# Twelve float32r products of a hidden tile, ordered by contraction piece instead of by operand pair

## The chip, the cores and the metric

The kernel runs on one core of a Trainium2 chip. The metric is the device time of one execution in microseconds (us). Three runs of the kernel before took 601.49, 601.64 and 602.29 us; the median is 601.64 us. For a measurement of this kernel, a difference under about 0.2% (1.2 us) is no difference.

## What is computed

Three layers follow one another. The first is chunked attention with eight memory slots (batch 4, 8 heads, 768 positions, head size 64). Its output, seen as 3072 tokens of 512 features, goes through a rational activation layer. The result goes through a soft mixture of experts.

```python
def _moe_ref(x, w_in, w_out, a, b):
    h = x @ w_in                      # 3072x512 @ 512x2048
    h2 = h * h
    h3 = h2 * h
    P = a[0] + a[1] * h + a[2] * h2 + a[3] * h3
    Q = 1.0 + np.abs(b[0]) * np.abs(h) + np.abs(b[1]) * h2
    g = P / (Q + 1e-06)
    return (g @ w_out).astype(np.float32)
```

The change touches `h = x @ w_in` alone.

## The kernel before, in words

The 3072 tokens are cut into six blocks of 512, and the 2048 hidden features into 8 steps of 256. So there are 48 steps, and each makes one h tile: 128 partitions by two halves of 512 tokens, in two PSUM banks. Two h tiles are alive at a time (pool `ps_h`, two buffers): the tile of the next step is computed while the activation works on that of the present one.

The product is made in float32r, in three parts. x is split into a high part `xh` and a low part `xl`, and `w_in` into `wh` and `wl`; h is the sum of `wh*xh`, `wh*xl` and `wl*xh`. The contraction is 512 long, that is four pieces `c` of 128. So a half of an h tile takes 3 x 4 = 12 matmuls, which accumulate in one bank (`h_part`, the matmul stands in line 321), and the kernel makes 48 x 2 x 12 = 1152 of them. In each, `ww[:, c, ...]` (128x128) is the operand that is loaded into TensorE and `xx[:, c, :]` (128x512) the one that is streamed. Before the change the twelve come in three groups of four: `wh*xh` for all c, then `wh*xl` for all c, then `wl*xh` for all c.

The parts come from elsewhere, and late in some places:

- `xh` and `xl` of a block are made by `attention`, in four slices of tokens, each over all four pieces. ScalarE copies a slice out of PSUM as `xh` (line 237), and VectorE then subtracts it from the same PSUM tile to make `xl` (line 238). Before the first h tile of a new block is computed (in step 7 of the block before), the rest of the attention is emitted.
- `wh` and `wl` of a step are made once, in block 0: ScalarE rounds the converted weight to `wh` (line 304), VectorE makes `wl` from the difference (line 305).

TensorE also makes the transposes of the activation result (line 347, copied out by ScalarE in line 348), the logits (line 340), the attention (lines 164, 201, 214, 233), and in block 0 a product of `w_out` with `phi` (lines 416, 424). All of those but line 340 write to three PSUM banks of the pool `ps_m`, shown as tile `m`. The activation is done by ScalarE (lines 540, 541, 543, 559, 560), VectorE (542, 553, 554, 570, 571) and GpSimd (517). Line 540 is the first reader of a finished h tile. The steps' lists of words (`KN`) say in which order the parts of a step are emitted: `h0` and `h1` are the two halves, `at` a slice of attention, `p0` and `p1` the transposes. Behind the first stage, a scheduler lays out each engine's instructions ahead of time: by the order of emission, but with an instruction that isn't ready by its own estimate passed over for one that is. On the chip each engine then goes strictly by that layout.

Of the kernel before, what the change touches and what calls it, by code (L numbers as in the profile page):

```python
# [44 lines left out]
def tile_chunk_attention__rational__soft_moe(  # L45
# [30 lines left out]
    NC = DM // P  # L76
# [238 lines left out]
    def h_part(step, tile_, f2):  # L315
        b, i = divmod(step, NSTEP)
        (wh, wl), (xh, xl) = win[i], xt[b]
        n = 0
        for ww, xx in ((wh, xh), (wh, xl), (wl, xh)):
            for c in range(NC):  # L320
                PE.matmul(tile_[:, f2, :], lhsT=ww[:, c, f2 * P:f2 * P + P], rhs=xx[:, c, :],  # L321
                          start=(n == 0), stop=(n == 3 * NC - 1))
                n += 1
# [143 lines left out]

    hs[0] = ps_h("h", [P, 2, BLK])
    h_part(0, hs[0], 0)
    h_part(0, hs[0], 1)  # L470
    state = {"att": None}

# [49 lines left out]
    def run_step(kk, what):  # L522
# [5 lines left out]
        elif what in ("h0", "h1"):  # L528
            if nxt < total:
                if what == "h0":  # L530
                    if nxt % NSTEP == 0:
                        while state["att"] is not None:
                            slice_()
                    hs[nxt] = ps_h("h", [P, 2, BLK])
                h_part(nxt, hs[nxt], int(what[1]))
# [231 lines left out]
```

## Time and profile before

| | |
|---|---|
| median of three runs | 601.64 us |
| span of the profiled execution, first to last instruction | 599.9 us |
| TensorE matmul busy | 541.6 us (90%) |
| TensorE weight load busy | 382.6 us (64%) |
| VectorE busy | 455.1 us (76%) |
| ScalarE busy | 417.3 us (70%) |
| GpSimd busy | 125.3 us (21%) |

The profile is of one execution. Its span runs from the first to the last instruction; the metric's 601.64 us is 1.7 us more, for what lies around it. In the trace, a matmul of this kernel shows as two records: one on PEld (the load of its 128x128 operand into TensorE) and one on PE (the streaming of the other operand and the drain of the result). Records on PE overlap, since the next product starts before the last one has drained: what a product costs in a row of them is the distance from its start to that of the next.

### The profile page before, as it was taken

Reading aid. Unit: us, or ns where it says so; the run is one execution under the profiler, and the core shown is the slowest. Engines: PE = TensorE matmul, PEld = TensorE weight load, DVE = VectorE, ACT = ScalarE, POOL = GpSimd, SP = SyncE. Lnnn points to the kernel's source line nnn. Section 1 sums busy time; section 2 is a strip of 40 time slices with the busy share of each in tenths; the row PEclk is TensorE's granted clock in tenths of the full one; section 3 lists DMA queues with packets and bytes.
Section 4 is the critical chain, followed back from the end, with each engine's and each line's share of the span. In section 5 each row is a group of like instructions: output and inputs, shape, how many; then the busy total and the mean of one; then the engine's idle time right before and its main releaser. Section 6 shows DMA issues by size and latency. Waiting matters only on the chain.

```text
span 599.9 us, 13580 instructions
## 1 busy us (share of the span) xinstructions
PE 541.6 (90%) x5898; PEld 382.6 (64%) x5898; DVE 455.1 (76%) x561; ACT 417.3 (70%) x542; POOL 125.3 (21%) x65
## 2 busy tenths in 40 slices
PE   2679899989999999999999999999999999779982
PEld 2567766657767777677776777766777576326241
DVE  4667999988987988978889698896987968711032
ACT  2468999987877868778687777777787869510032
POOL 0000132113313133131331313132232225200000
PEclk9779999989999999999999999999999999889996
DMA  7975987230221223212122022210274334799949
GB/s 298 413 277 188 350 293 261 80 132 0 108 72 32 76 71 107 71 29 79 72 107 69 7 103 73 106 68 5 106 272 157 134 107 174 283 352 410 409 185 360
DMA packets 21755, 97.41 MB, mean 162 GB/s; under 512 B 3136, under 2 KB 3136, under 8 KB 16704
## 3 DMA queue, kind: packets, MB, share of 16 engines
q1 hardware_dynamic: 19728, 92.28, 41.8%
q0 software_dynamic: 1152, 4.19, 1.7%
q8 instruction: 46, 0.75, 0.5%
q10 hardware_dynamic: 816, 0.07, 0.1%
q14 instruction: 13, 0.11, 0.0%
HBM read 86.05 MB, written 10.49 MB: 161 GB/s over the span
## 4 chain that ended last, share of the span: by engine, by line
PE 53%; ACT 19%; DVE 13%; DMA 5%; issue 5%; POOL 2%; SPq 0%; ACTq 0%; DVEq 0%; POOLq 0%
PE h L321 27%; PE m L398 4%; ACT S L540 4%; ACT S L541 3%; PE m L347 3%; ACT g L348 3%; PE lg L340 3%; PE m L214 3%; DVE T L553 3%; PE h L640 2%; PE m L233 2%; POOL S L517 2%; PE m L201 2%; DMA xt<-in_kw_dram 2%; DVE T L554 2%
## 5 line engine op out<-in xcount | busy, mean ns | idle before, releaser
L321 PE MATMUL h<-xt,win 128*128 128x512 f32 x1152 | 294.2, 403 | 7.2 <-ACT win L304 5.1
L321 PEld LDWEIGHTS h<-xt,win 128*128 128x128 f32 x1152 | 210.7, 190 | 54.9 <-ACT win L304 7.7
L517 POOL TENSOR_TENSOR S<-S,S 128x1024 f32<-128x1024 f32 (+1 forms) x49 | 118.9, 2428 | 315.9 <-DVE S L542 302.9
L540 ACT ACTIVATE S<-h,ctab 128x1024 f32<-128x1024 f32 (+1 forms) x49 | 54.0, 1102 | 57.5 <-PE h L321 55.4
L542 DVE SCALAR_TENSOR_TENSOR S<-S,S 128x1024 f32<-128x1024 f32 (+1 forms) x49 | 58.8, 1199 | 41.6 <-ACT S L541 41.4
L553 DVE TENSOR_TENSOR T<-T,h 128x1024 f32<-128x1024 f32 (+1 forms) x49 | 58.4, 1191 | 6.7 <-ACT T L543 6.7
L570 DVE SCALAR_TENSOR_TENSOR T<-T,ctab,S 128x1024 f32<-128x1024 f32 (+1 forms) x49 | 63.3, 1294 | 0.0
L571 DVE SCALAR_TENSOR_TENSOR T<-S,T 128x1024 f32<-128x1024 f32 (+1 forms) x49 | 59.8, 1220 | 3.2 <-POOL S L517 0.5
L347 PEld LDWEIGHTS m<-ident,T 128*128 128x128 f32 x384 | 44.1, 144 | 28.2 <-issue 14.2
L554 DVE SCALAR_TENSOR_TENSOR T<-T,ctab,h 128x1024 f32<-128x1024 f32 (+1 forms) x49 | 61.2, 1250 | 0.7
L543 ACT ACTIVATE T<-h,ctab 128x1024 f32<-128x1024 f32 (+1 forms) x49 | 59.3, 1210 | 0.0
L560 ACT ACTIVATE S<-S,ctab 128x1024 f32<-128x1024 f32 (+1 forms) x49 | 55.9, 1141 | 0.8
L559 ACT ACTIVATE S<-S 128x1024 f32<-128x1024 f32 (+1 forms) x49 | 51.8, 1056 | 6.8 <-DVE S L542 5.0
L348 ACT ACTIVATE g<-m 128x512 f32<-128x512 f32 x96 | 53.6, 605 | 3.1 <-PE m L347 2.9
L347 PE MATMUL m<-ident,T 128*128 128x128 f32 x384 | 54.2, 281 | 1.4 <-DVE a L185 1.2
L541 ACT ACTIVATE S<-h,ctab 128x1024 f32<-128x1024 f32 (+1 forms) x49 | 54.3, 1107 | 0.5 <-DVE T L570 0.5
L340 PE MATMUL lg<-T,wp 128*32 128x512 f32 x192 | 39.9, 614 | 5.4 <-DVE T L571 5.4
L398 PE MATMUL m<-g,ptok 128*32 128x512 f32 x192 | 23.5, 634 | 0.4 <-ACT ptok L390 0.4
L186 ACT ACTIVATE a<-a 128x512 f32<-128x512 f32 x22 | 13.9, 643 | 14.1 <-DVE a L185 14.1
L214 PE MATMUL m<-v,a 64*32 64x64 f32 x1408 | 20.5, 229 | 3.0 <-issue 2.8
L238 DVE TENSOR_TENSOR xt<-m,xt 128x512 fp32r<-128x512 f32 x24 | 16.3, 687 | 7.9 <-ACT xt L237 7.8
L214 PEld LDWEIGHTS m<-v,a 64*32 64x32 f32 x1408 | 17.1, 108 | 7.4 <-issue 4.6
(158 smaller groups left out, 595.6 us busy)
## 6 DMA issues: line engine op xcount, KB each, us to landing
win<-in_moe_w_dram SPq DMA_DIRECT2D x32, 512.0 KB, 6.0
k<-in_kw_dram SPq DMA_DIRECT2D x11, 1024.0 KB, 7.5
v<-in_vw_dram SPq DMA_DIRECT2D x11, 1024.0 KB, 5.4
g<-in_moe_w_in_dram SPq DMA_DIRECT2D x8, 1024.0 KB, 6.2
g<-in_moe_w_out_dram SPq DMA_DIRECT2D x8, 1024.0 KB, 8.1
out_dram<-win SPq DMA_DIRECT2D x12, 512.0 KB, 5.0
q<-in_qw_dram SPq DMA_DIRECT2D x11, 512.0 KB, 3.9
T<-in_moe_w_dram SPq DMA_DIRECT2D x10, 512.0 KB, 9.7
```

The source lines that it names most:

```text
L321: PE.matmul(tile_[:, f2, :], lhsT=ww[:, c, f2 * P:f2 * P + P], rhs=xx[:, c, :], start=(n == 0), stop=(n == 3 * NC - 1))
L347: PE.transpose(pb[:, m, f2 * P:f2 * P + P], t_[:, f2, tt * P:tt * P + P], ident)
L348: ACT.activation(gts[b, qd][:, 2 * part:2 * part + 2, 2 * P * o:2 * P * o + 2 * P], pb, AF.Copy)
L517: POOL.tensor_tensor(out[:, o], q[:, o], w[:, o], ALU.mult)
L540: ACT.activation(s[:, o], hh[:, o], AF.Abs, scale=b0)
L541: ACT.activation(y[:, o], hh[:, o], AF.Square, scale=rb1)
L542: DVE.scalar_tensor_tensor(s[:, o], y[:, o], QC, s[:, o], ALU.add, ALU.add)
L543: ACT.activation(t[:, o], hh[:, o], AF.Identity, bias=a2, scale=a3)
L553: DVE.tensor_tensor(t[:, o], t[:, o], hh[:, o], ALU.mult)
L554: behind[kk] = DVE.scalar_tensor_tensor(t[:, o], t[:, o], a1, hh[:, o], ALU.add, ALU.mult).ins
L570: DVE.scalar_tensor_tensor(t[:, o], t[:, o], a0, w[:, o], ALU.add, ALU.mult)
L571: DVE.scalar_tensor_tensor(t[:, o], e[:, o], 2.0, t[:, o], ALU.subtract, ALU.mult, reverse0=True)
```

## The change

The two loops around the matmul change places: the piece `c` of the contraction is the outer loop, and the three pairs are the inner one. The twelve products, their operands and the bank are the same; their order is `wh*xh`, `wh*xl`, `wl*xh` for c = 0, then the same for c = 1, 2 and 3.

```diff
--- before.py
+++ after.py
@@ -316,8 +316,8 @@
         b, i = divmod(step, NSTEP)
         (wh, wl), (xh, xl) = win[i], xt[b]
         n = 0
-        for ww, xx in ((wh, xh), (wh, xl), (wl, xh)):
-            for c in range(NC):
+        for c in range(NC):
+            for ww, xx in ((wh, xh), (wh, xl), (wl, xh)):
                 PE.matmul(tile_[:, f2, :], lhsT=ww[:, c, f2 * P:f2 * P + P], rhs=xx[:, c, :],
                           start=(n == 0), stop=(n == 3 * NC - 1))
                 n += 1
```

## Rows read from the trace of the kernel before

**Rows 1.** Stretches: us, busy and count by engine, granted clock, DMA share, GB/s.

```profile
36.70:142.00 105.30, 96.58 (x988) 72.95 (x989) 91.98 (x100) 90.81 (x114) 21.00 (x14) 0.96 0.57 201
142.00:218.00 76.00, 75.59 (x885) 54.84 (x883) 63.92 (x77) 59.79 (x75) 19.22 (x8) 1.00 0.20 71
218.00:294.00 76.00, 75.75 (x890) 55.28 (x885) 65.36 (x79) 59.55 (x78) 19.27 (x8) 1.00 0.21 71
```

**Rows 2.** Waits of ScalarE, 142 to 508 us: total, times, longest.

```profile
ACT S L540 <- PE h L321: 54.0, 25, 3.6
```

**Rows 3.** Waits of ScalarE in block 0, 36.7 to 142 us.

```profile
ACT S L540 <- PE h L321: 1.5, 1, 1.5
```

**Rows 4.** The page's costliest groups: busy, mean ns, idle before; the products' own.

```profile
L321 PE MATMUL h<-xt,win 128*128 128x512 f32 x1152 | 294.2, 403 | 7.2 <-ACT win L304 5.1
L321 PEld LDWEIGHTS h<-xt,win 128*128 128x128 f32 x1152 | 210.7, 190 | 54.9 <-ACT win L304 7.7
```

**Rows 5.** Timeline of PE: start us, duration us; single products, and a long row.

```profile
225.77 0.50 PE L321 MATMUL h<-xt,win 128*128 128x512 f32 x1
...
226.11 0.40 PE L321 MATMUL h<-xt,win 128*128 128x512 f32 x1
...
139.62 6.74 PE L321 MATMUL h<-xt,win 128*128 128x512 f32 x29
```

**Rows 6.** Groups by shape, line 698 (tile m): loads and matmuls.

```profile
L698 PE MATMUL m<-s,call 32*128 32x256 f32 x48 | 8.8, 402 | 0.5 <-DVE win L705 0.5
...
L698 PEld LDWEIGHTS m<-s,call 32*128 32x128 f32 x48 | 6.8, 184 | 1.2 <-DVE win L705 0.9
```

**Rows 7.** Timeline of PE, the second and the ninth product of the first half tile.

```profile
37.29 0.63 PE L321 MATMUL h<-xt,win 128*128 128x512 f32 x1
...
40.28 0.63 PE L321 MATMUL h<-xt,win 128*128 128x512 f32 x1
```

**Rows 8.** The stretch that holds both, with the granted clock.

```profile
36.70:40.70 4.00, 4.00 (x9) 3.13 (x10) 2.94 (x3) 2.08 (x2) 0.73 (x1) 0.50 0.33 55
```

**Rows 9.** Timeline around the first h tile of block 2 (in brackets: idle, releaser).

```profile
218.19 0.63 ACT L237 ACTIVATE xt<-m 128x512 fp32r<-128x512 f32 x1
...
219.29 5.76 PE L321 MATMUL h<-xt,win 128*128 128x512 f32 x24
219.50 0.68 DVE L238 TENSOR_TENSOR xt<-m,xt 128x512 fp32r<-128x512 f32 x1
...
220.24 4.39 PEld L321 LDWEIGHTS h<-xt,win 128*128 128x128 f32 x20 [0.21 <-DVE xt L238]
220.70 0.64 ACT L348 ACTIVATE g<-m 128x512 f32<-128x512 f32 x1
...
222.22 0.65 ACT L348 ACTIVATE g<-m 128x512 f32<-128x512 f32 x1
...
225.15 1.12 ACT L540 ACTIVATE S<-h,ctab 128x1024 f32<-128x1024 f32 x1 [2.28 <-PE h L321]
```

**Rows 10.** The second and the fifth product of that h tile, alone.

```profile
219.60 0.39 PE L321 MATMUL h<-xt,win 128*128 128x512 f32 x1
...
220.30 0.45 PE L321 MATMUL h<-xt,win 128*128 128x512 f32 x1
```

**Rows 11.** Timeline of block 0, step 7, and the first h tile of block 1.

```profile
128.51 1.46 PE L321 MATMUL h<-xt,win 128*128 128x512 f32 x3 [0.45 <-ACT win L304]
...
130.16 1.41 PE L321 MATMUL h<-xt,win 128*128 128x512 f32 x5
...
131.14 1.28 DVE L238 TENSOR_TENSOR xt<-m,xt 128x512 fp32r<-128x512 f32 x2
...
135.73 2.58 DVE L305 TENSOR_TENSOR win<-g,win 128x1024 fp32r<-128x1024 f32 x1
...
138.36 9.36 PE L321 MATMUL h<-xt,win 128*128 128x512 f32 x40 [0.47 <-DVE win L305]
...
142.32 1.12 ACT L540 ACTIVATE S<-h,ctab 128x1024 f32<-128x1024 f32 x1 [1.86 <-PE h L321]
```

**Rows 12.** Timeline of block 0, step 3.

```profile
69.27 1.23 DVE L305 TENSOR_TENSOR win<-g,win 128x1024 fp32r<-128x1024 f32 x1
69.29 1.89 PE L321 MATMUL h<-xt,win 128*128 128x512 f32 x7 [2.36 <-ACT win L304]
...
71.11 1.48 PE L214 MATMUL m<-v,a 64*32 64x64 f32 x128
```

**Rows 13.** Timeline of VectorE just before the first h tile of all.

```profile
35.94 1.43 DVE L238 TENSOR_TENSOR xt<-m,xt 128x512 fp32r<-128x512 f32 x2 [1.35 <-ACT xt L237]
```

## The prediction

> **What bounds the kernel now.** First I read the stretches, each engine's busy time in each. From 142 us on, the kernel repeats itself block by block in 76 us, and TensorE is busy in 75.59 and 75.75 of 76.0 us, at the full granted clock, while VectorE and ScalarE have 11 to 16 us to spare [rows 1]. Then the waits: from 142 to 508 us the longest wait of ScalarE is for a finished h tile, 25 times and 54.0 us in sum [rows 2]. So in blocks 1 to 5 the products of the h tile are the bound, and what TensorE loses there the kernel loses. Block 0 is another thing: 105.3 us, TensorE idle in 8.7 of them, and ScalarE waited for an h tile just once, for 1.5 us [rows 1, 3]. There the weights are converted, and TensorE has some slack.
>
> Last I read what one product costs. There are 1152, each with a load of its own: 1152 load records of 190 ns beside 1152 matmuls [rows 4]. In an undisturbed row, 29 products take 6.74 us from the first's start to the last's end; less the last one's own record of 0.39 us, 28 distances take 6.35, or 0.227 us from start to start [rows 5, 10]. A load of 0.19 us fits into that; it runs beside the product before. Only the second product of a row pays: it starts 0.34 us after the first (225.77 to 226.11), 0.113 more than the pace [rows 5].
>
> **The change part by part.** It removes and adds no instruction. It does two things.
>
> *Equal operands in a row.* In each group of three the second product has the loaded operand of the first, so 4 of 12, 384 of 1152, could do without a load. Nothing in the edit takes the load out: it is the same matmul call, which brings its load. The nearest row is line 698, where two matmuls after one another in the code have the same loaded operand: 48 matmul records, 48 load records [rows 6]. It is near but not equal, since such a plain f32 product shows as two matmul records with a load each, so equal loads aren't next to each other. I take the loads to stay and the pace to stay 0.227: no gain. The other bound is what a dropped load could give. At half clock the products come (40.28 - 37.29) / 7 = 0.427 us apart [rows 7, 8]; if all of it is streaming, it is 0.2136 at the full clock, and 0.013 of the 0.227 is not streaming. 384 x 0.013 = 5.0 us, and the second product of a row would save 0.113 as well. With a row per step (48) that is 5.4 us more, with a row per half (96) 10.8. So between 0 and -15.8 us; I take 0, the row with a load for each matmul being nearest.
>
> Here a page speaks for a gain. The Trainium skill (TensorE: Matmul & The Clock Gate, Step-by-step: what each phase is for) says that weights stay put over many matmuls, and that load and compute are separate so that one can load once and multiply repeatedly; by that the sum would be 4.35 - 10.4 = -6.05 us. No row here shows a matmul without its load.
>
> *Operands needed earlier.* The first `xl` was needed by the fifth product and is now needed by the second; the first `wl` was needed by the ninth and is now needed by the third. That matters where they arrive late. Products queue in order, so those behind the waiting one wait too.
>
> Block starts 2 to 5 (four, alike; one stands in the rows). The first product starts at 219.29 with `xh` just ready, the second at 219.60; VectorE makes the last `xl` from 219.50 to 220.18, and the first product that reads it, the fifth, starts at 220.30, right after its load was held by that [rows 9, 10]. `xl` was thus already the last to arrive, hidden under four products. After the change the second product takes that place: 220.30 instead of 219.60, so three products come out from under the cover, 0.70 us. The tile ends that much later, ScalarE is waiting for it already (2.28 us) [rows 9], and TensorE has no idle time in the block to give back [rows 1]. 4 x 0.70 = 2.8 us. Block start 1 pays nothing: its `xl` was done at 132.42, its first product comes behind 138.36 [rows 11].
>
> Step 7 of block 0. `wh` let the products begin at 128.51; eight (3 + 5) ran; `wl` was made only from 135.73 to 138.31, and 40 products then followed without a break [rows 11]. Now just two can run ahead, so six more stand behind 138.36: 6 x 0.227 = 1.36 us. ScalarE waits for the following tile (1.86 us before 142.32), and there the TensorE-bound part begins, so I count it in full.
>
> The first half tile of all: the last `xl` ends at 37.37 [rows 13], the second product started at 37.29 [rows 7]; with 0.11 from the end of `xl` to the product, +0.19 us.
>
> Steps 3 to 6 of block 0 (alike, one shown): the products begin at 69.29, `wl` is done at 70.50 [rows 12]. The third product would have come at 69.29 + 0.34 + 0.23 = 69.86 and now comes at 70.61, +0.75; four times that is 3.0 us. I cost it at nothing, because in block 0 ScalarE doesn't wait for h tiles [rows 3] and TensorE has other work to put in between, as the 128 small attention products at 71.11. Without this cover it is +3.0. Steps 1 and 2 have their `wl` in time. Buffers are freed as before, since the last product of a half reads `wl` and `xh` in either order; DMA queues don't move.
>
> The sum: 2.8 + 1.36 + 0.19 = +4.35 us. The profiled execution spans 599.9 us, the runs' median is 1.7 us more for what lies around it; 599.9 + 1.7 + 4.35 = 606.0 us. The bounds of this case are +1.4 (block starts recovered elsewhere) and +7.35 (steps 3 to 6 uncovered): 603.0 to 609.0.
>
> **The rivals.**
>
> *Nothing measurable: the scheduler fills the new gap.* It lays out TensorE's work by estimated readiness; in block 0 it cut rows of products apart for other work [rows 11, 12]. If it puts other work after the first product at the block starts, the gap is used and only the broken row costs 4 x 0.113 = 0.45; if the backlog of step 7 finds slack as well, what is left is 0.5 us: 602.1. Against it: at 219.3 to 220.2 the three `m` banks have readers to come (line 238 until 220.18, line 348 at 220.70 and 222.22 [rows 9]), so transposes and attention have nowhere to write.
>
> *Faster: the load is dropped or costs nothing when repeated.* Place: every second product of a group of three. Price: -5.0 - 5.4 = -10.4 us against +4.35 of waits, 595.6 us; it decides as soon as a repeated load saves more than 4.35 / 384 = 11 ns. For it: the pace is 0.013 us above streaming, and something must take that. Against it: loads equal matmuls in number wherever I look [rows 4, 6].
>
> *Faster by a new layout.* The dependences of two products in each half move, and the layout of all later work follows from the estimate. If each of 48 steps had one broken row fewer, 48 x 0.113 = 5.4 us come back, more than the waits: 600.6 us. As well it could be a break more, 611.4. Nothing in the trace prefers a side.
>
> **How the numbers follow.** A measurement can tell 0.2%, 1.2 us, from no change. My forecast, waits uncovered, has 0.60 and lies wholly on the slower side (603.0 to 609.0). Nothing measurable: 0.20. The dropped load: 0.08. The new layout: 0.08 faster, 0.04 slower. So faster 0.16, same 0.20, slower 0.64. The range must leave out at most 0.2: I leave out the dropped load and the slow layout (0.12) and reach down into the fast layout, to 599.5, and up to 609.0.
>
> **What the profile will show.** Right: 1152 loads beside 1152 products, a pace of 0.227 in undisturbed rows; at the starts of blocks 2 to 5 the second product about 1.0 us after the first, held by line 238; in block 0 two products ahead of the `wl` of step 7 and 22 behind it; blocks of about 76.7 us where a wait is, 76.0 otherwise. Wrong: fewer loads than products, a pace near 0.214, a second product of a row at 0.23 instead of 0.34; or TensorE's order around the block starts cut up with other work, and blocks of 76.0 us or less; or blocks that are longer with no wait of TensorE in them.

## The result, and the profile after

The changed kernel takes 610.34 us (median of four runs, 609.44 to 610.47), against 601.96 us for the kernel before in the same comparison: ratio 1.0135, 95% interval 1.0121 to 1.0150, so 8.4 us slower. The profiled execution spans 608.7 us against 599.9. The prediction had the side right and two of the three places (+4.35 us, 606.0), but its range ended at 609.0.

First, the loads. The page's costliest groups of the changed kernel answer to [rows 4]:

```profile
L321 PE MATMUL h<-xt,win 128*128 128x512 f32 x1152 | 297.1, 404 | 8.3 <-ACT win L304 3.4
L321 PEld LDWEIGHTS h<-xt,win 128*128 128x128 f32 x1152 | 211.4, 190 | 58.9 <-ACT win L304 5.5
```

There is still one load of 190 ns for each of the 1152 products. The timeline of PE (start us, duration us) shows the pace: in an undisturbed row, and at the start of a row.

```profile
231.99 0.50 PE L321 MATMUL h<-xt,win 128*128 128x512 f32 x1
...
232.32 0.39 PE L321 MATMUL h<-xt,win 128*128 128x512 f32 x1
...
467.25 4.93 PE L321 MATMUL h<-xt,win 128*128 128x512 f32 x21
```

(4.93 - 0.39) / 20 = 0.227 us, as in [rows 5]; and the second product of a row, which now has the loaded operand of the first, still starts 0.33 us behind it. Nothing was gained from equal operands.

The lost time is in two places. One is the start of each block from the second on; the timeline around the first h tile of block 2 answers to [rows 9]:

```profile
224.80 0.48 PE L321 MATMUL h<-xt,win 128*128 128x512 f32 x1
225.01 0.68 DVE L238 TENSOR_TENSOR xt<-m,xt 128x512 fp32r<-128x512 f32 x1
...
225.75 5.52 PE L321 MATMUL h<-xt,win 128*128 128x512 f32 x23 [0.47 <-DVE xt L238]
...
231.37 1.12 ACT L540 ACTIVATE S<-h,ctab 128x1024 f32<-128x1024 f32 x1 [2.99 <-PE h L321]
```

The second product follows the first after 0.95 us, held by line 238; the tile takes 225.75 + 5.52 - 224.80 = 6.47 us where it took 5.76, so +0.71, and ScalarE's wait for it grew from 2.28 to 2.99, by the same 0.71. In the waits of ScalarE from 148 to 515 us, the line that answers to [rows 2] has grown by 5.4 us:

```profile
ACT S L540 <- PE h L321: 59.4, 25, 4.7
```

Four such tiles are 2.8 us of that; the rest is the wait for the tile at the end of block 0, which grew from 1.86 to 4.69 us. That wait leads to the other place, block 0, and above all its step 7. The timeline there, which answers to [rows 11]:

```profile
130.40 0.70 PE L321 MATMUL h<-xt,win 128*128 128x512 f32 x2
...
131.49 1.05 PE L340 MATMUL lg<-T,wp 128*32 128x512 f32 x4
...
136.97 1.91 PE L424 MATMUL m<-u,S 128*128 128x32 f32 x8 [2.52 <-ACT S L417]
...
137.64 2.56 DVE L305 TENSOR_TENSOR win<-g,win 128x1024 fp32r<-128x1024 f32 x1
...
141.90 4.35 PE L321 MATMUL h<-xt,win 128*128 128x512 f32 x15
...
147.87 1.12 ACT L540 ACTIVATE S<-h,ctab 128x1024 f32<-128x1024 f32 x1 [4.69 <-PE h L321]
```

Two products run ahead of `wl`, as predicted. But `wl` is there at 140.20 and the third product starts at 141.90: TensorE isn't waiting for `wl` any more, it is late itself. The stretches tell why. Of the changed kernel (us, busy by engine in the order PE, PEld, DVE, ACT, POOL, then the granted clock):

```profile
130.40:136.50 6.10, 3.30 (x21) 1.68 (x19) 3.56 (x4) 6.10 (x9) 0.53 (x1) 1.00 0.22 89
136.50:143.30 6.80, 6.33 (x27) 6.07 (x28) 6.69 (x6) 4.19 (x7) 2.35 (x1) 0.50 0.00 0
```

The same two stretches of the kernel before:

```profile
128.50:134.60 6.10, 6.04 (x24) 3.34 (x24) 4.15 (x5) 6.10 (x9) 0.53 (x1) 0.91 0.22 89
134.60:138.40 3.80, 2.87 (x25) 2.63 (x25) 3.80 (x4) 2.05 (x5) 2.36 (x1) 1.00 0.00 0
```

Before, six more products filled the time ahead of `wl`: TensorE was busy in 6.04 of 6.10 us. Now it is busy in 3.30 of them, with one wait of 2.52 us, and the clock granted after that is 0.50, 1.2 GHz instead of 2.4, for 6.8 us. Of the kernel before:

```profile
131.50 1.05 PE L340 MATMUL lg<-T,wp 128*32 128x512 f32 x2
...
133.50 1.04 PE L340 MATMUL lg<-T,wp 128*32 128x512 f32 x2
...
135.06 1.08 PE L424 MATMUL m<-u,S 128*128 128x32 f32 x8 [0.52 <-ACT S L417]
...
136.23 0.98 PE L424 MATMUL m<-u,S 128*128 128x32 f32 x8
```

The six products are only 1.36 of the 2.74 us of missing work; another 1.04 us is missing because the four logits of line 340 now run in one row of 1.05 us, where before two and two took 1.05 and 1.04. At half clock the eight small products of line 424 take 1.91 us (1.08 before), and the next eight 1.75 (0.98), so the queue ahead of the third product runs late. From the end of `wl` to the activation's start it was 142.32 - 138.31 = 4.01 us [rows 11]; it is now 147.87 - 140.20 = 7.67. That is +3.66 us where the prediction had +1.36.

`wl` itself is late, too. Line 305 for step 2, changed kernel (for step 7 it stands above, at 137.64):

```profile
56.42 1.23 DVE L305 TENSOR_TENSOR win<-g,win 128x1024 fp32r<-128x1024 f32 x1 [0.26 <-ACT win L304]
```

That is 81.22 us from the one to the other. In the kernel before it was 135.73 - 56.71 = 79.02 us ([rows 11], and this line):

```profile
56.71 1.23 DVE L305 TENSOR_TENSOR win<-g,win 128x1024 fp32r<-128x1024 f32 x1 [0.27 <-ACT win L304]
```

So steps 3 to 6 lost 2.20 us, which the prediction had put at nothing. In steps 5 and 6 of the changed kernel the third product waits for `wl`, and no other work stands in between:

```profile
98.52 0.73 PE L321 MATMUL h<-xt,win 128*128 128x512 f32 x2 [0.90 <-ACT win L304]
99.77 1.66 PE L321 MATMUL h<-xt,win 128*128 128x512 f32 x6 [0.52 <-DVE win L305]
...
113.88 0.73 PE L321 MATMUL h<-xt,win 128*128 128x512 f32 x2 [0.53 <-DVE win L305]
```

And around the `wl` of step 3 (68.95 us) the clock is at half. Stretch 69 to 75 us, first the kernel before, then the changed one:

```profile
69.00:75.00 6.00, 5.71 (x146) 4.54 (x146) 5.86 (x10) 6.00 (x8) 0.04 (x1) 1.00 0.77 279
```

```profile
69.00:75.00 6.00, 5.96 (x136) 4.25 (x137) 6.00 (x9) 6.00 (x8) 0.38 (x1) 0.50 0.66 201
```

The sum by these rows: 2.20 + 3.66 + 4 x 0.71 = 8.70 us, against 8.4 us between the medians and 8.8 between the two profiled spans.

### The profile page after: what moved, and what is told of

Its sections match the earlier page's. It is cut to its first block, busy times and chain, and to the rows that moved or that the text cites. A ratio compares the mean times of both kernels' runs of the same rounds, so it can differ in the third digit from the quotient of the medians.

```text
span 608.7 us, 13576 instructions
## 1 busy us (share of the span) xinstructions
PE 547.9 (90%) x5898; PEld 386.2 (63%) x5898; DVE 455.5 (75%) x561; ACT 417.5 (69%) x542; POOL 125.2 (21%) x65
## 3 DMA queue, kind: packets, MB, share of 16 engines
q0 software_dynamic: 1152, 4.19, 1.7%
## 4 chain that ended last, share of the span: by engine, by line
PE 54%; ACT 17%; DVE 14%; DMA 5%; issue 5%; POOL 2%; SPq 0%; ACTq 0%; DVEq 0%; POOLq 0%
PE h L321 28%; PE m L398 4%; ACT S L540 4%; ACT S L541 3%; PE m L214 3%; PE m L347 3%; ACT g L348 3%; DVE S L542 3%; DVE T L553 2%; PE lg L340 2%; PE h L640 2%; PE m L424 2%; DVE T L554 2%; POOL S L517 2%; PE m L201 2%
```

## The experiments

Each kernel differs in the order of the twelve products alone, unless said otherwise. The order is a list of (piece, loaded operand, streamed operand), and the diffs, against the changed kernel, show that list. They are shortened: `by pair` stands for the list of the kernel before and `by piece` for that of the change, and the loop that makes the products from the list is left out. Medians move by about 1 us from one comparison to the next, so the ratios, each against the kernel before on the same chip, are what is compared.

**Only xl early.**

```diff
+order = [(c, wh, xx) for c in range(NC) for xx in (xh, xl)]
+order += [(c, wl, xh) for c in range(NC)]
```

> Only xl is needed early (second product); wl is needed from the ninth product on, as before the change. Theory of the late operands: only the four block starts pay, 4 x 0.65 us, plus at most 0.2 at the first tile: 604.6 to 604.9 us against 602.0 before, ratio about 1.0045, and step 7 of block 0 ends about where it did before. Rival, equal loaded operands in a row cost time themselves (four of twelve products have them here too): about 610, ratio 1.014. Pace in undisturbed rows 0.227 by the first, over 0.230 by the second.

Measured: 605.26 us, ratio 1.0039 (1.0024 to 1.0054). The first theory holds for the time. A third of the products have the loaded operand of their forerunner here, just as in the change, and yet more than two thirds of the change's loss is gone. But step 7 didn't end as it did before:

```profile
132.30:138.40 6.10, 5.08 (x32) 3.15 (x32) 5.06 (x6) 4.51 (x6) 2.75 (x2) 1.00 0.22 89
138.40:141.90 3.50, 3.50 (x13) 2.74 (x13) 3.50 (x3) 3.21 (x5) 0.13 (x1) 0.52 0.00 0
```

```profile
137.05 2.56 DVE L305 TENSOR_TENSOR win<-g,win 128x1024 fp32r<-128x1024 f32 x1
...
144.69 1.12 ACT L539 ACTIVATE S<-h,ctab 128x1024 f32<-128x1024 f32 x1 [2.91 <-PE h L321]
```

Here, too, the clock was about half when `wl` came, although eight products had run ahead of it and TensorE had been busy in 5.08 of the 6.10 us before; the activation came 144.69 - 139.61 = 5.08 us after `wl` instead of 4.01. The full gap of the old order does not rule out the half clock.

**Only wl early.**

```diff
+order = [(c, ww, xh) for c in range(NC) for ww in (wh, wl)]
+order += [(c, wh, xl) for c in range(NC)]
```

> Only wl is needed early (second product); xl is needed from the ninth product on; no two products in a row have the same loaded operand. Theory of the late operands: block 0 pays as it does with the change (step 7 ends 5.5 us later than before, about 147.8 us), the block starts pay nothing: 602.0 + 5.5 - 0.2 = 607.3 us, ratio about 1.009; maybe 0.5 us more, since one product fewer runs ahead of wl. Rival, equal loaded operands cost: 602, ratio 1.000.

Measured: 607.05 us, ratio 1.0071 (1.0050 to 1.0091). No equal operands in a row, and still slower by 4.3 us; the waits at the block starts are gone, the first h tile of block 2 is again a row of 24 products in 5.73 us:

```profile
224.92 5.73 PE L321 MATMUL h<-xt,win 128*128 128x512 f32 x24
```

**The new order only where nothing is late** (35 of 48 steps).

```diff
-order = by piece, in all steps
+order = by pair, as before
+if b and i:
+    order = by piece
```

> The new order only in the 35 steps where all operands are long there (blocks 1 to 5 without each block's first step); block 0 and each block's first step as before the change. Theory of the late operands: nothing changes, 602.0 us, ratio 0.999 to 1.001, 1152 loads, pace 0.227. Rival, equal loaded operands cost 10 ns each: 280 pairs, +2.9 us, ratio 1.005. Rival, a repeated load is dropped or cheaper: faster by up to 3.6 us, ratio 0.994.

Measured: 602.86 us, ratio 1.0006 (0.9991 to 1.0021), against 602.92 in the same comparison. Of its page:

```profile
L322 PE MATMUL h<-xt,win 128*128 128x512 f32 x1152 | 293.0, 402 | 7.0 <-ACT win L304 4.8
L322 PEld LDWEIGHTS h<-xt,win 128*128 128x128 f32 x1152 | 210.5, 189 | 54.1 <-ACT win L304 7.5
```

Both rivals fall: 280 equal operands in a row neither cost nor give anything that can be measured. Where every operand is there in time, the new order is free.

**By piece, but with no equal operands in a row.**

```diff
-for ww, xx in ((wh, xh), (wh, xl), (wl, xh)):
+for ww, xx in ((wh, xh), (wl, xh), (wh, xl)):
```

> By piece of the contraction first as in the change, but inside a piece wh*xh, wl*xh, wh*xl, so no product has the loaded operand of the one before it, while late operands are needed at nearly the same places (wl second, xl third). Theory of the late operands: at the block starts one product more runs ahead, 4 x 0.23 less; in step 7 one product fewer, 0.23 more, a little more in steps 3 to 6: 609.5 to 611 us, ratio 1.012 to 1.015. Rival, equal loaded operands cost: 602 + 4.4 = 606.4 us, ratio 1.007.

Measured: 609.30 us, ratio 1.0111 (1.0091 to 1.0131). Its middle lies just under what was expected, and the rival's 1.007 is outside the interval.

**The change, with step 7 of block 0 in the old order.**

```diff
+if step == 7:
+    order = by pair, as before
```

> The change, with step 7 of block 0 alone in the old order, so that eight products run ahead of its late wl. Theory: the 3.65 us that this step lost against before come back (six products, and the time at the low clock that their absence brought): 610.3 - 3.6 = 606.7 us, ratio 1.008. Rival, the loss is in the waits of steps 3 to 6 and only shows up at step 7: 1.4 us or less comes back, 609 us, ratio 1.0117.

Measured: 606.21 us, ratio 1.0068 (1.0046 to 1.0090); against the change's 1.0135 that is 0.67% of 602, 4.0 us back. From its timeline:

```profile
137.98 2.56 DVE L305 TENSOR_TENSOR win<-g,win 128x1024 fp32r<-128x1024 f32 x1
...
144.56 1.12 ACT L540 ACTIVATE S<-h,ctab 128x1024 f32<-128x1024 f32 x1 [1.85 <-PE h L322]
```

144.56 - 140.54 = 4.02 us from `wl` to the activation, as in the kernel before (4.01).

**The change, with six idle products in step 7.** They compute nothing that is used: the twelve that follow write over them.

```diff
+if step == 7 and f2 == 0:
+    for c in (0, 1, 2, 3, 0, 1):
+        PE.matmul(tile_[:, f2, :], lhsT=wh[:, c, 0:P], rhs=xh[:, c, :], start=True, stop=True)
 order = by piece
```

> The change, with six extra products (wh*xh, their result is overwritten) ahead of the twelve of the first half of step 7 of block 0. They do no useful work, they only keep TensorE busy where the old order had six real products. Theory: the half clock from 136.5 to 143.3 us doesn't come, TensorE reaches the waiting third product right when wl is there, and 1.65 us (late third product) + 0.64 us (slow products after it) come back: 608.0 us, ratio 1.010. Rival, the clock falls anyway or is not what made the third product late: 610.3 us or up to 1.4 more.

Measured: 608.10 us, ratio 1.0100 (1.0083 to 1.0116), 2.1 us back, from a kernel that does more work. Its stretches and timeline:

```profile
131.00:137.00 6.00, 5.69 (x26) 3.11 (x24) 3.78 (x5) 6.00 (x9) 0.53 (x1) 0.97 0.23 90
137.00:141.00 4.00, 3.30 (x26) 3.02 (x27) 4.00 (x3) 2.25 (x5) 2.35 (x1) 1.00 0.00 0
```

```profile
137.92 2.56 DVE L305 TENSOR_TENSOR win<-g,win 128x1024 fp32r<-128x1024 f32 x1
...
140.53 5.74 PE L323 MATMUL h<-xt,win 128*128 128x512 f32 x24 [0.46 <-DVE win L305]
...
145.85 1.12 ACT L541 ACTIVATE S<-h,ctab 128x1024 f32<-128x1024 f32 x1 [3.21 <-PE h L323]
```

With TensorE busy ahead of `wl`, the clock stays at 1.00, the third product starts 0.05 us after `wl`, and it is 145.85 - 140.48 = 5.37 us to the activation: 1.36 more than before. That is the predicted 6 x 0.227 for the six products that stand behind `wl`. The other 7.67 - 5.37 = 2.30 us of step 7 are what the idle time and the half clock behind it cost.

**The changed kernel once more.**

> The changed kernel once more, for a second profile of it. If the half clock at 68 to 75 us and at 136.5 to 143.3 us belongs to the change, both are there again; if it is the luck of one execution, one or both are missing, and the span is shorter by the 0.7 us (the first) or 2.3 us (the second) that they cost.

Measured: one run, 610.80 us, span 609.0. Both half-clock stretches are there again:

```profile
69.00:75.00 6.00, 5.96 (x136) 4.25 (x137) 6.00 (x9) 6.00 (x8) 0.42 (x1) 0.50 0.64 202
136.90:143.70 6.80, 6.52 (x28) 6.23 (x29) 6.69 (x5) 4.00 (x7) 2.35 (x1) 0.50 0.00 0
```

**The change, with steps 3 to 6 in the old order.**

```diff
+if step in (3, 4, 5, 6):
+    order = by pair, as before
```

> The change, with steps 3 to 6 of block 0 alone in the old order. In the profile of the change, step 7 begins 1.9 us later than before, although the start of step 3 was 0.3 earlier: 2.2 us were lost in steps 3 to 6. Theory: these come back, 608.1 us, ratio 1.010. Rival, they are the luck of when the clock fell (it was half from 68 to 75 us in that one execution and not before): nothing comes back on the median, 610.3 us, ratio 1.0135.

Measured: 608.21 us, ratio 1.0106 (1.0087 to 1.0125), 1.7 us back. From line 305 of step 2 to that of step 7 it is 79.01 us again, as before the change, so the 2.2 us of the profile belong to the order of these steps:

```profile
56.53 1.23 DVE L305 TENSOR_TENSOR win<-g,win 128x1024 fp32r<-128x1024 f32 x1 [0.30 <-ACT win L304]
...
135.54 2.56 DVE L305 TENSOR_TENSOR win<-g,win 128x1024 fp32r<-128x1024 f32 x1
```

**Step 3 alone, and steps 4 to 6 alone, in the old order.**

```diff
+if step == 3:            # the other kernel: step in (4, 5, 6)
+    order = by pair, as before
```

> The change, with step 3 of block 0 alone in the old order. In both profiles of the changed kernel the half clock came at 68 us and stayed 6.8 us, and step 3 lost 1.2 to 1.4 us between its start and its end. Theory, most of what steps 3 to 6 lost is lost in step 3: 1.2 us come back, 609.1 us, ratio 1.0115. Rival, every one of the four loses alike: 0.5 us, 609.8 us.

> The change, with steps 4, 5 and 6 of block 0 in the old order: the rest of the 2.1 us. If step 3 holds most, 0.9 us come back, 609.4 us, ratio 1.0125; if the four are alike, 1.6 us, 608.7 us, ratio 1.011.

Measured: 607.54 us, ratio 1.0078 (1.0063 to 1.0093) with step 3; 608.76 us, ratio 1.0097 (1.0082 to 1.0112) with steps 4 to 6. That is 3.4 and 2.3 us back, where all four steps together gave 1.7. I missed both: the steps don't add up. The profiles say the same, of step 3 first, then of steps 4 to 6:

```profile
57.35 1.22 DVE L305 TENSOR_TENSOR win<-g,win 128x1024 fp32r<-128x1024 f32 x1 [0.32 <-ACT win L304]
...
135.01 2.56 DVE L305 TENSOR_TENSOR win<-g,win 128x1024 fp32r<-128x1024 f32 x1
```

```profile
57.31 1.23 DVE L305 TENSOR_TENSOR win<-g,win 128x1024 fp32r<-128x1024 f32 x1 [0.27 <-ACT win L304]
...
137.06 2.56 DVE L305 TENSOR_TENSOR win<-g,win 128x1024 fp32r<-128x1024 f32 x1
```

From step 2 to step 7 it is 77.66 us with step 3 put back and 79.75 with steps 4 to 6, against 81.22 in the change and 79.02 before it. So the new order of steps 4 to 6 alone made this stretch 1.36 us shorter than before, although their waits of 0.5 us for `wl` are there (at 98.44 and 112.55), and that of step 3 alone 0.73 longer; only both together cost 2.20.

The clock has a share in it. Five kernels have all of steps 3 to 6 in the changed order. Where the granted clock from 68 to 76 us was 0.57 (the change, its second profile, and the kernel of the block starts below), the distance is 81.22, 81.48 and 81.58 us; where it was 0.79 (step 7 put back, and the idle products), 80.50 and 80.45. With step 3 put back it was 0.79 as well, so the clock isn't all of it. The rest of TensorE's work is laid out differently in block 0, too: the logits near 82 us stand in one row before the change and with step 3 put back, and in two in the change. How waits, clock and layout divide the 2.2 us stays open.

**The change, with each block's first step in the old order.**

```diff
+if b and i == 0:
+    order = by pair, as before
```

> The change, with the first step of blocks 1 to 5 in the old order. Theory of the late xl: 4 x 0.65 = 2.6 us come back, 607.7 us, ratio 1.0093, and the second product of those tiles follows the first after 0.31 us instead of 0.95. Together with step 7 (4.1) and steps 3 to 6 (2.1) that would be 8.8 us, against 8.4 for the whole change.

Measured: 607.23 us, ratio 1.0069 (1.0047 to 1.0091): 4.0 us back, more than expected, with a wide interval. The first tile of block 2:

```profile
225.36 5.76 PE L322 MATMUL h<-xt,win 128*128 128x512 f32 x24
```

5.76 us again, as in [rows 9]. The rest of the 4.0 us came back behind the last product, where the changed order has no part. The products' line (duration ns, first and last start), first of the changed kernel, then of this one:

```profile
L321 PE MATMUL h<-xt,win x1152: 387/389/796, 36.0 to 514.5; 128*128 128x512 f32 x192
```

```profile
L322 PE MATMUL h<-xt,win x1152: 387/389/796, 35.7 to 512.4; 128*128 128x512 f32 x192
```

From the last start to the end it is 608.7 - 514.5 = 94.2 us in the one and 605.0 - 512.4 = 92.6 in the other (599.9 - 506.3 = 93.6 in the kernel before). Over all profiles the closing stage takes from 92.4 us (only `wl` early) to 94.8 us (no equal operands in a row), and why was not followed up; the 1.6 us here are a quarter of a per cent, and what a kernel gives back is not known better than that.

**The opposite of the change.** On the kernel before: where an operand is late, its products go behind those of both halves of the tile (`wl` in block 0, `xl` in the first step of each later block), so that sixteen products instead of eight can run ahead.

```diff
+first, late = ((wh, xh), (wh, xl)), (wl, xh)
+if b and i == 0:
+    first, late = ((wh, xh), (wl, xh)), (wh, xl)
+order = [(f2, c, ww, xx) for ww, xx in first for c in range(NC)]
+if not (b == 0 or i == 0):
+    order += [(f2, c, *late) for c in range(NC)]
+elif f2:
+    order += [(f, c, *late) for f in range(2) for c in range(NC)]
```

> Not the change, but its opposite, on the kernel before: where an operand is late, its products are put behind those of both halves of the h tile (wl in block 0, xl in the first step of each later block). In step 7 sixteen products instead of eight can run ahead of wl. If the time goes with what is left behind the late operand: 8 x 0.227 = 1.8 us less in step 7 and 4 x 0.06 at the block starts, 600.0 us against 602.0, ratio 0.9967. Rival: in block 0 ScalarE and the late wl set the pace and the layout puts other work in between anyway: 0.998 to 1.001.

Measured: 599.96 us, ratio 0.9953 (0.9941 to 0.9965): 2.8 us faster than the kernel before, and the fastest of all. Its step 7:

```profile
132.44 1.41 PE L328 MATMUL h<-xt,win 128*128 128x512 f32 x5
...
135.71 2.56 DVE L305 TENSOR_TENSOR win<-g,win 128x1024 fp32r<-128x1024 f32 x1
...
140.51 1.12 ACT L546 ACTIVATE S<-h,ctab 128x1024 f32<-128x1024 f32 x1
```

The last of the sixteen products run by 133.85, 1.86 us before VectorE even begins `wl`. 140.51 - 138.27 = 2.24 us remain from `wl` to the activation, 1.77 less than the 4.01 of the kernel before, for eight products fewer (8 x 0.227 = 1.82). The expected ratio, 0.9967, lies just outside the interval. The profiled span, 597.9 us, is 2.0 us shorter than before, as was expected; where the rest of the 2.8 us is was not found.

## Why the prediction was right and wrong

**What bounds the kernel: right.** In blocks 1 to 5 a tile that ended 0.71 us later made ScalarE wait 0.71 us longer.

**No gain from equal operands: right.** 1152 loads, pace 0.227, second product of a row at 0.33, and ratio 1.0006 where only this part of the change is at work. The rival with the dropped load falls.

**Block starts, 4 x 0.70: right.** 0.71 per tile, gone where each block's first step is in the old order. The rival that the scheduler fills this gap falls: the row of 23 products follows the wait directly.

**Step 7 of block 0, six products behind `wl`: right in kind, too small.** The six cost 1.36 us, to the hundredth; the step cost 3.66. What failed is the sentence that priced the six products only where they now stand. They were also the work that had kept TensorE busy where they stood before: without them its clock fell to half, and the work queued ahead of the third product ran late. The prediction had no term for the granted clock here and didn't ask what would keep it full. The kernel with six idle products shows this part by itself, 2.30 us. All eight profiles with one or two products ahead of this `wl` have half clock somewhere between 131 and 146 us; of the six with eight or more (in one of them six are the idle ones), five have none, and the one with only `xl` early has it. So an emptier gap went with the lower clock, but the fuller one was no guarantee.

**Steps 3 to 6 at nothing: wrong.** The cover named (ScalarE doesn't wait for h tiles there, TensorE has other work) didn't hold: in steps 5 and 6 TensorE stood idle for `wl`, 0.52 and 0.53 us, with no other work put in between, and the four steps lost 2.20 us, inside the bound of +3.0 that the prediction had kept. Nor can the four be summed step by step, as that bound was: step 3 and steps 4 to 6, put back by themselves, gave 3.4 and 2.3 us, both together 1.7.

**The first half tile, +0.19:** not told apart from the variation of the early part between profiles, in which line 305 of step 2 starts anywhere from 56.28 to 58.01 us.

**The range.** Its upper end, 609.0, stood for uncovered steps 3 to 6 with everything else as priced. It had no term for the clock; without the 2.3 us of clock in step 7 the result would have been inside. The new layout as a cause falls for blocks 1 to 5, where TensorE's groups of instructions come in the order of before. In block 0 they don't, and there it is not ruled out: the 1.36 us that the new order of steps 4 to 6 alone gave, in one profile, may be its work.

## What to carry to other kernels

When products of one accumulation are reordered, list for each operand when it is ready and what now stands behind it; put the products of the operand that comes last at the end, over as many accumulators as are open. And where products are taken out of a gap, they can cost twice, once behind the gap and once through TensorE's clock, if it falls when the gap is emptier; look at the granted clock of the stretch, and not just at who waits.

## What I had not expected of the hardware

After a stretch with 3.30 us of matmuls in 6.10, and a longest wait of 2.52 us, TensorE was granted half its clock for 6.8 us, though it was busy in 6.33 of these. With six matmuls more in that gap, whose result nobody reads, the clock stayed at 1.00 and the kernel was 2.1 us faster. And in one kernel the clock was about half for 3.5 us after a stretch with 5.08 us of matmuls in 6.10.
